# Token tiles of a fused linear-attention and gMLP kernel: transposed by TensorE, or loaded transposed and centred by an adding transfer

## The chip, the cores and the metric

The kernel runs on one NeuronCore of a Trainium2 chip. The metric is device time in microseconds (us), from the first instruction to the last with what lies around it. The kernel before takes 641.28 us (median of 3 runs, 640.76 to 642.08).

Five engines run side by side, each in its own fixed order: TensorE (PE in the profile, with its weight loads as PEld), VectorE (DVE), ScalarE (ACT), GpSimd (POOL) and SyncE (SP), which only issues transfers. GpSimd and ScalarE also issue transfers. An instruction waits on semaphores of other engines and of transfers, and everything behind it on its engine waits with it.

## The reference

One layer of 2048 tokens with 512 features, in float32. Cut to what matters:

```python
x  = A_x                                          # [1, 2048, 512]
xn = layernorm(x)                                 # per token: (x - mean) / sqrt(var + 1e-5)
out = x + A(xn) + B(xn)

def A(x):                                         # linear attention, 32 heads of 16
    q, k, v = split(x @ wqkv)
    pq, pk  = per_head(q) @ w_phi, per_head(k) @ w_phi
    phi_q = concat(softmax(pq), softmax(-pq));  phi_k likewise
    kv, z = phi_k^T v, sum over tokens of phi_k
    return ((phi_q kv) / (phi_q z + 1e-6)) @ wo

def B(x):                                         # gated MLP over tokens
    z1, z2 = halves(gelu(x @ w_in))               # 688 columns each
    g = w_sp @ layernorm(z2) + b_sp               # [2048, 2048] over the tokens
    return (z1 * g) @ w_out
```

## The kernel before, in words

Tokens are cut into 16 tiles of 128. Every product is made in three passes of float32r numbers (a high part times a high part, high times low, low times high: `mm3`, lines 50 to 53), so each operand is split into a high part `h` (a rounding copy, line 43) and a rest `l` (a subtraction, line 47).

The first stage, up to about 225 us, is where the change lies. For each tile `s` it needs the tile transposed (features on the 128 partitions) and with each token's mean taken off; the factor 1/sqrt(var) is applied later, to the outputs. A tile goes through these steps:

- `fetch` (line 176 by way of `load_x`): SyncE loads `xt`, tokens on partitions. Five buffers (`XB`).
- `stats` (lines 249, 250): VectorE finds mean and variance of each token.
- `center` (lines 254 to 256): GpSimd makes `nm`, the negative mean, and r = 1/sqrt(var + eps) (lines 84, 85); ScalarE adds `nm` to `xt`.
- `transposed` (line 268): four 128x128 transposes on TensorE into a PSUM bank `pt`.
- `split_x`: ScalarE rounds `pt` to the high part of `xT` (line 43), VectorE takes the rest (line 47).

Tiles 0 to 3 are done in a hand-written prologue, with the loading and folding of the weights. A loop over `s` does the others. Pass `s` of the loop has the projection to keys `proj` of tile `s` (12 matrix multiplications of 128x512), the softmax pair `softmax_k` on it (lines 103 to 113: max and min, two subtractions, `Exp` on ScalarE, sum, reciprocal), `normalise` (lines 285, 286: VectorE scales the features `e`, and GpSimd issues a transfer that adds them to `zacc`), the projection to values of tile `s + 1`, statistics and centring of tile `s + 3`, a projection to queries with its softmax pair whose result GpSimd writes to `e_d` (line 281), and a projection `zps` for the gated MLP (line 140). After each even `s`, `run` puts the transposes of tiles `s + 2` and `s + 3` and then the products `kvps` of features and values (line 293) on TensorE, and after them the two splits. Key, value and query projections and the transposes share four PSUM banks (tag `mm`).

The order on each engine is set by the program's own scheduler from its cost estimates; `issue_after` binds some instructions behind others. The input `x_t`, the tokens in transposed blocks, is an argument of the kernel before as well, which does not read it.

Behind the first stage come the rest of the MLP projections, a Strassen-like product over the tokens (`g`, from about 290 to 500 us), and the output projections. They are the same in both kernels.

Of the kernel before, what the change touches and what calls it, by code (L numbers as in the profile page):

```python
# [10 lines left out]
F32 = mybir.dt.float32  # L11
# [7 lines left out]
P = 128  # L19
# [10 lines left out]
XB = 5  # L30
# [5 lines left out]
def mixer(ctx: ExitStack, tc: tile.TileContext, x, x_t, wv, wqkT, phi_bd, wo, w_in, wst, b_r, w_out, out):  # L36
# [34 lines left out]
    zb_d = dram.tile([P, NF], F32, name="zb_d")  # L71

# [8 lines left out]
    def rstd_of(mv, r, stats=None):  # L81
        if stats is not None:
            dve.bn_aggr(mv, stats)
        pool.tensor_scalar_add(mv[:, 1:2], mv[:, 1:2], EPS_LN)
        pool.tensor_tensor(r, mv[:, 1:2], mhalf, op=ALU.pow)
# [83 lines left out]
    with ExitStack() as p0:  # L169
# [87 lines left out]

        def centered_on_dve(s):
            stats(s)
            ins = dve.tensor_scalar(xt[s], xt[s], mv_x[:, s, 0:1], None, op0=ALU.subtract).ins  # L260
            rstd_of(mv_x[:, s], r_x[:, s:s + 1])
            return ins
# [20 lines left out]
        def normalise(er):  # L283
            e = er[:, :NF]
            dve.tensor_tensor(heads(e), heads(e), bc(er[:, NF:], 2 * H), op=ALU.mult)
            pool.dma_start(zacc, e, accum_op=ALU.add)
            return e
# [9 lines left out]
        def run(tiles, feats):  # L297

            with ExitStack() as order:
                for i in ahead_of_run:  # L300
                    order.enter_context(tc.issue_after(i))
                ahead_of_run.clear()
                pts = []
                for t in tiles:
                    pt, i = transposed(t)
                    pts.append(pt)
                    order.enter_context(tc.issue_after(i))
                for t, e in feats:
                    i = add_kv(t, e)
            for pt in pts:  # L310
                split_x(pt)
            return i
# [9 lines left out]
        fetch(4)  # L322
        w1r = load_rows(w_in[:, :FH], FH)
        sp.dma_start(bias, b_r)
# [75 lines left out]
        for s in range(NT):  # L400
            if s:
                fetch(s + 4)
            er = ek if s == 0 else softmax_k(s, p1 if s == 1 else proj(s, wqk_h[:, 1], wqk_l[:, 1]))
            ahead_of_run.append(proj.last)
            feats.append((s, normalise(er)))
            if 0 < s < NT - 1:
                ahead_of_run.append(proj_v(s + 1)[0])
            if 0 < s < NT - 3:
                with tc.issue_after(shifted):
                    stats(s + 3)  # L410
                with tc.issue_after(z1_raw.last if s % 2 and s > 1 else q_half):
                    center(s + 3)
# [13 lines left out]
            if s and s % 2 == 0:  # L426
                last = run([t for t in (s + 2, s + 3) if t < NT], feats[:-1])
# [527 lines left out]
```

## Time and profile before

| | |
|---|---|
| median of 3 runs | 641.28 us (640.76 to 642.08) |
| the profiled execution | 639.98 us, of which the span 638.3 us |
| TensorE busy | 632.3 us, 99% of the span |
| VectorE busy | 507.1 us, 79% |
| ScalarE busy | 273.4 us, 43% |
| GpSimd busy | 105.7 us, 17% |
| granted TensorE clock | full in all 40 slices of the span |

How to read it: the span is one execution, taken by the hardware profiler. A group line of the profile gives the source line, engine, operation and tile names (output <- inputs), how often it ran, busy time and mean duration, then the idle time in front of it and what ended that. A timeline row gives start and duration in us. A transfer's issue is a short instruction on the engine that issues it; its landing is told apart. Instructions of VectorE and ScalarE overlap by some 0.1 us at their ends, so steps between starts are a little shorter than durations.

### The profile page before, as it was taken

Reading aid. Unit: us, or ns where it says so; the run is one execution under the profiler, and the core shown is the slowest. Engines: PE = TensorE matmul, PEld = TensorE weight load, DVE = VectorE, ACT = ScalarE, POOL = GpSimd, SP = SyncE. Lnnn points to the kernel's source line nnn. Section 1 sums busy time; section 2 is a strip of 40 time slices with the busy share of each in tenths; the row PEclk is TensorE's granted clock in tenths of the full one; section 3 lists DMA queues with packets and bytes.
Section 4 is the critical chain, followed back from the end, with each engine's and each line's share of the span. In section 5 each row is a group of like instructions: output and inputs, shape, how many; then the busy total and the mean of one; then the engine's idle time right before and its main releaser. Section 6 shows DMA issues by size and latency. Waiting matters only on the chain.

```text
span 638.3 us, 11615 instructions
## 1 busy us (share of the span) xinstructions
PE 632.3 (99%) x4511; PEld 574.9 (90%) x4511; DVE 507.1 (79%) x919; ACT 273.4 (43%) x457; POOL 105.7 (17%) x194
## 2 busy tenths in 40 slices
PE   8999999999999999999999999999999999999997
PEld 6898888888888999999999999999999887888886
DVE  6979789888978579889988778687796698989521
ACT  5533433343332447887534434434343433223330
POOL 4532211212101005432010010100101200001000
PEclk9999999999999999999999999999999999999999
DMA  8363543534453851002453443533548877775620
GB/s 334 120 163 82 148 141 96 163 106 109 126 170 91 275 195 67 0 2 67 135 193 102 146 148 104 178 125 118 163 149 273 278 264 246 259 278 194 240 68 33
DMA packets 38519, 98.15 MB, mean 154 GB/s; under 512 B 4832, under 2 KB 6368, under 8 KB 38464
## 3 DMA queue, kind: packets, MB, share of 16 engines
q1 hardware_dynamic: 26720, 55.46, 27.0%
q0 software_dynamic: 9152, 35.79, 18.1%
q10 hardware_dynamic: 2592, 6.16, 2.5%
q8 instruction: 35, 0.57, 0.4%
q14 instruction: 20, 0.16, 0.1%
HBM read 56.24 MB, written 26.48 MB: 130 GB/s over the span
## 4 chain that ended last, share of the span: by engine, by line
PE 97%; DMA 2%; DVE 0%; SPq 0%; ACT 0%; issue 0%; POOL 0%
PE g L53 11%; PE g L52 11%; PE g L51 11%; PE proj L51 7%; PE proj L52 7%; PE proj L53 7%; PE zps L51 6%; PE zps L53 6%; PE zps L52 6%; PE pout L51 6%; PE pout L52 5%; PE pout L53 5%; PE ptq L828 1%; PE po L842 1%; PE kvps L293 1%; PE pout L860 1%
## 5 line engine op out<-in xcount | busy, mean ns | idle before, releaser
L53 PE MATMUL g<-B,A 128*128 128x344 f32 x448 | 143.4, 320 | 0.0
L52 PE MATMUL g<-B,A 128*128 128x344 f32 x448 | 143.3, 320 | 0.0
L51 PE MATMUL g<-B,A 128*128 128x344 f32 x448 | 143.3, 320 | 0.0
L53 PEld LDWEIGHTS g<-B,A 128*128 128x128 f32 x448 | 84.2, 188 | 0.1
L51 PEld LDWEIGHTS g<-B,A 128*128 128x128 f32 x448 | 84.2, 188 | 0.0
L52 PEld LDWEIGHTS g<-B,A 128*128 128x128 f32 x448 | 84.2, 188 | 0.0
L43 ACT ACTIVATE A<-S 128x512 fp32r<-128x512 f32 x64 | 39.9, 630 | 61.9 <-PE g L53 32.6
L47 DVE TENSOR_TENSOR A<-S,A 128x512 fp32r<-128x512 f32 x64 | 43.6, 687 | 27.6 <-ACT A L43 27.1
L110 ACT ACTIVATE e<-e,r_x 128x1024 f32<-128x1024 f32 x32 | 36.8, 1150 | 50.0 <-DVE e L109 34.8
L112 DVE TENSOR_REDUCE sm<-e 128x64 f32<-128x1024 f32 x32 | 38.7, 1210 | 15.0 <-ACT e L110 15.0
L51 PE MATMUL proj<-wqk_h,xT 128*128 128x512 f32 x124 | 49.6, 400 | 0.0
L52 PE MATMUL proj<-wqk_l,xT 128*128 128x512 f32 x124 | 48.7, 393 | 0.0
L53 PE MATMUL proj<-wqk_h,xT 128*128 128x512 f32 x124 | 48.7, 393 | 0.0
L43 ACT ACTIVATE A<-wf 128x512 fp32r<-128x512 f32 x64 | 33.3, 520 | 34.3 <-PE g L53 29.1
L47 DVE TENSOR_TENSOR A<-wf,A 128x512 fp32r<-128x512 f32 x64 | 35.4, 553 | 9.8 <-ACT A L43 9.3
L51 PE MATMUL zps<-w_h,xT 128*128 128x344 f32 x128 | 41.8, 326 | 0.0
L53 PE MATMUL zps<-w_h,xT 128*128 128x344 f32 x128 | 40.9, 319 | 0.0
L52 PE MATMUL zps<-w_l,xT 128*128 128x344 f32 x128 | 40.8, 319 | 0.0
L140 ACT ACTIVATE z1f<-zps,r_x 128x344 f32<-128x344 f32 (+1 forms) x29 | 16.5, 576 | 40.4 <-PE zps L53 37.8
L51 PE MATMUL pout<-wu,uh 128*128 128x512 f32 (+1 forms) x80 | 31.6, 395 | 0.0
L52 PE MATMUL pout<-wu,uh 128*128 128x512 f32 (+1 forms) x80 | 30.4, 380 | 0.0
L53 PE MATMUL pout<-wu,ul 128*128 128x512 f32 (+1 forms) x80 | 30.4, 380 | 0.0
(197 smaller groups left out, 1461.5 us busy)
## 6 DMA issues: line engine op xcount, KB each, us to landing
wf<-in_wst SPq DMA_DIRECT2D x64, 256.0 KB, 3.3
e_d<-e POOLq DMA_DIRECT2D x16, 544.0 KB, 3.2
et<-e_d SPq DMA_DIRECT2D x16, 544.0 KB, 5.6
zacc<-e POOLq DMA_DIRECT2D x16, 512.0 KB, 4.6
er<-et POOLq DMA_DIRECT2D x12, 512.0 KB, 3.9
u_d<-z1t POOLq DMA_DIRECT2D x16, 368.0 KB, 4.9
u<-u_d SPq DMA_DIRECT2D x15, 368.0 KB, 4.7
z_d<-z1f ACTq DMA_DIRECT2D x16, 344.0 KB, 4.0
```

The lines of the kernel that those rows point to most:

```text
L43: return act.activation(h, src, AF.Copy).ins
L47: return (eng or dve).tensor_tensor(l, src, h.bitcast(F32), op=ALU.subtract).ins
L51: pe.matmul(dst, ah, bh, start=start, stop=False)
L52: pe.matmul(dst, ah, bl, start=False, stop=False)
L53: return pe.matmul(dst, al, bh, start=False, stop=stop).ins
L110: act.activation(e, e, AF.Exp, scale=scale)
L112: dve.tensor_reduce(sm, heads(e), axis=AX.X, op=ALU.add)
L140: z1_raw.last = act.activation(z[:, k], p, AF.Copy, scale=r_x[:, s:s + 1]).ins
L293: ins = pe.matmul(kv_acc[k:k + QP, m // 4], vs[:, m * QP:(m + 1) * QP], e[:, m * HP:(m + 1) * HP], start=s == 0 and m < 4, stop=s == NT - ...
L828: pe.transpose(pt[:, a, k].bitcast(F32R), src, ident_r)
L842: lasts[3] = pe.matmul(po[r][c * QP:(c + 1) * QP, j // NG], kvT[rows, j], fs[j // 2][rows, j % 2], start=True, stop=True).ins
L860: pe.matmul(p, rt, w[:, ds], start=False, stop=False)
```

## The change

From the fifth tile on (tiles 4 to 15), the tile is no longer transposed and centred on the chip's engines:

- `fetch_T` loads the tile twice: `xt` as before, for the statistics alone (three buffers now), and `raw` from `x_t`, already in transposed blocks (two buffers, the pool's default).
- `mean_out` (in place of `center`): GpSimd makes the negative means `nm` and writes them, 128 numbers, to `nm_d` in device memory.
- `mean_in`: after the transfer that adds the features to `zacc`, GpSimd issues a second adding transfer. It reads the row of 128 means for each of 128 partitions and 4 blocks and adds it to `raw`.
- `split_x` then splits `raw` (in SBUF) instead of `pt` (in PSUM), one tile a pass, two tiles ahead.
- `run` has only the products `kvps`; the 48 transposes of tiles 4 to 15 and the 12 centrings on ScalarE are gone.

```diff
-XB = 5
+XB = 3
...
+    nm_d = dram.tile([NT, P], F32, name="nm_d")
...
-        pool.tensor_tensor(r, mv[:, 1:2], mhalf, op=ALU.pow)
+        return pool.tensor_tensor(r, mv[:, 1:2], mhalf, op=ALU.pow).ins
...
+        raws = {}
+
+        def fetch_T(s):
+            if s < NT:
+                fetch(s)
+                raws[s] = wk.tile([P, ND, P], F32, tag="raw", name="raw")
+                sp.dma_start(raws[s], x_t[s])
+
+        def mean_out(s):
+            stats(s)
+            xt.pop(s)
+            nm = wk.tile([P, 1], F32, tag="nm", name="nm")
+            pool.tensor_scalar_mul(nm, mv_x[:, s, 0:1], -1.0)
+            pool.dma_start(nm_d[s:s + 1, :].rearrange("a p -> p a"), nm)
+            return rstd_of(mv_x[:, s], r_x[:, s:s + 1])
+
+        def mean_in(s):
+            pool.dma_start(raws[s], nm_d[s:s + 1, :].unsqueeze(1).to_broadcast([P, ND, P]), accum_op=ALU.add)
+
...
-            pool.dma_start(zacc, e, accum_op=ALU.add)
+            normalise.last = pool.dma_start(zacc, e, accum_op=ALU.add).ins
...
-        def run(tiles, feats):
+        def run(feats):
...
-                pts = []
-                for t in tiles:
-                    pt, i = transposed(t)
-                    pts.append(pt)
-                    order.enter_context(tc.issue_after(i))
                 for t, e in feats:
                     i = add_kv(t, e)
-            for pt in pts:
-                split_x(pt)
             return i
...
-        fetch(4)
         w1r = load_rows(w_in[:, :FH], FH)
+        fetch_T(4)
...
         for s in range(NT):
-            if s:
-                fetch(s + 4)
             er = ek if s == 0 else softmax_k(s, p1 if s == 1 else proj(s, wqk_h[:, 1], wqk_l[:, 1]))
             ahead_of_run.append(proj.last)
+            if 1 < s < NT - 2:
+                with tc.issue_after(shifted):
+                    split_x(raws.pop(s + 2))
+            if s:
+                fetch_T(s + 4)
             feats.append((s, normalise(er)))
             if 0 < s < NT - 1:
                 ahead_of_run.append(proj_v(s + 1)[0])
             if 0 < s < NT - 3:
                 with tc.issue_after(shifted):
-                    stats(s + 3)
-                with tc.issue_after(z1_raw.last if s % 2 and s > 1 else q_half):
-                    center(s + 3)
+                    mean_out(s + 3)
+                with tc.issue_after(normalise.last):
+                    mean_in(s + 3)
...
-                last = run([t for t in (s + 2, s + 3) if t < NT], feats[:-1])
+                last = run(feats[:-1])
```

The scheduler moves the instructions with it. Three places matter below. In each, rows are source line, operation, output <- inputs and the shape.

VectorE in the fourth and fifth pass, from the scaling of the key features of tile 4 (L285 before, L305 now) to those of tile 5. Before:

```order
L285 TENSOR_TENSOR e<-e 128x1024
L47 TENSOR_TENSOR xT<-pt,xT 128x512 x2
L112 TENSOR_REDUCE sm<-e 128x64
L103 TENSOR_REDUCE mm<-proj 128x32
L113 RECIPROCAL e<-sm 128x64
L104 TENSOR_REDUCE mm<-proj 128x32
L108 TENSOR_TENSOR e<-proj,mm 128x32x16
L109 TENSOR_TENSOR e<-mm,proj 128x32x16
L249 BN_STATS st_1021<-xt 128x6
L250 BN_AGGR mv_x<-st_1021 128x2
L112 TENSOR_REDUCE sm<-e 128x64
```

The same place in the change, as far as the sum over the key features of tile 5:

```order
L305 TENSOR_TENSOR e<-e 128x1024
L113 TENSOR_REDUCE sm<-e 128x64
L104 TENSOR_REDUCE mm<-proj 128x32
L105 TENSOR_REDUCE mm<-proj 128x32
L114 RECIPROCAL e<-sm 128x64
L109 TENSOR_TENSOR e<-proj,mm 128x32x16
L110 TENSOR_TENSOR e<-mm,proj 128x32x16
L250 BN_STATS st_1024<-xt 128x6
L251 BN_AGGR mv_x<-st_1024 128x2
L47 TENSOR_TENSOR xT<-raw,xT 128x512
L113 TENSOR_REDUCE sm<-e 128x64
```

Two splits of `pt` stood right behind the scaling in every second pass; now one split of `raw` (tile 7 here) stands in every pass, behind the statistics and ahead of the sum over this pass's key features. On ScalarE the rounding half of that split stands ahead of the `Exp` that this sum reads.

GpSimd in the same pass, from the negative means of one tile to the write of the query features. Before:

```order
L254 TENSOR_SCALAR nm<-mv_x 128x1
L84 TENSOR_SCALAR mv_x<-mv_x 128x1
L85 TENSOR_TENSOR r_x<-mv_x,mhalf 128x1
L286 DMA zacc<-e 128x1024
L281 DMA e_d<-e 128x1088
```

The same in the change:

```order
L271 TENSOR_SCALAR nm<-mv_x 128x1
L85 TENSOR_SCALAR mv_x<-mv_x 128x1
L272 DMA nm_d<-nm 128x1
L86 TENSOR_TENSOR r_x<-mv_x,mhalf 128x1
L306 DMA zacc<-e 128x1024
L276 DMA raw<-nm_d 128x4x128
L301 DMA e_d<-e 128x1088
```

The write of the means comes in behind `nm`, and the adding transfer to `raw` directly behind the one to `zacc`.

TensorE at the first of these tiles, from the end of the key projection of tile 3 to the value projection of tile 4. Before:

```order
L53 MATMUL proj<-wqk_h,xT 128x512
L51 MATMUL proj<-wv_h,xT 128x512
L52 MATMUL proj<-wv_l,xT 128x512
L51 MATMUL zps<-w_h,xT 128x344
L52 MATMUL zps<-w_l,xT 128x344
L53 MATMUL zps<-w_h,xT 128x344
L51 MATMUL zps<-w_h,xT 128x344
L52 MATMUL zps<-w_l,xT 128x344
L53 MATMUL proj<-wv_h,xT 128x512
```

The same in the change:

```order
L53 MATMUL proj<-wqk_h,xT 128x512
L51 MATMUL proj<-wv_h,xT 128x512
L52 MATMUL proj<-wv_l,xT 128x512
L53 MATMUL proj<-wv_h,xT 128x512
L51 MATMUL proj<-wv_h,xT 128x512
```

The five multiplications of the MLP projection that stood inside the value projection are now in one block with the rest of theirs, later.

## The prediction, made before the result was known

> **What bounds the kernel now.** I read the page's busy shares and its chain of waits first, then the first stage by windows, then row by row.
>
> ```profile
> span 638.3 us, 11615 instructions
> PE 632.3 (99%) x4511; PEld 574.9 (90%) x4511; DVE 507.1 (79%) x919; ACT 273.4 (43%) x457; POOL 105.7 (17%) x194
> PE 97%; DMA 2%; DVE 0%; SPq 0%; ACT 0%; issue 0%; POOL 0%
> ```
>
> TensorE carries 97% of the chain: a matrix instruction that goes is worth its place, and a wait costs its length. The ten passes from the key projection of tile 3 to that of tile 13 (columns: window, length, busy us of PE, PEld, DVE, ACT, POOL, clock, share of the DMA engines, GB/s), and TensorE at their ends:
>
> ```profile
> 43.04:168.71 125.67, 125.67 (x919) 107.72 (x913) 110.72 (x167) 48.48 (x65) 24.89 (x48) 1.00 0.46 128
> ...
> 41.04 1.04 PE L268 MATMUL pt<-ident,xt 128*128 128x128 f32 x8
> 42.01 1.10 PE L293 MATMUL kvps<-e,v 128*32 128x64 f32 x64
> 43.04 0.50 PE L51 MATMUL proj<-wqk_h,xT 128*128 128x512 f32 x1
> ...
> 168.71 0.50 PE L51 MATMUL proj<-wqk_h,xT 128*128 128x512 f32 x1
> ```
>
> TensorE is busy in all of it: 12.57 us a pass. VectorE has 110.72 of 125.67 us, 88%, so 1.5 us a pass are free on it; ScalarE is idle most of the time. TensorE waits for nobody here, but VectorE is the engine that would hold it next. One pass of VectorE, and the rows by which the steps are priced:
>
> ```profile
> 46.13 0.69 DVE L103 TENSOR_REDUCE mm<-proj 128x32 f32<-128x512 f32 x1 [1.92 <-PE proj L53]
> 46.74 0.68 DVE L104 TENSOR_REDUCE mm<-proj 128x32 f32<-128x512 f32 x1
> 47.33 0.68 DVE L108 TENSOR_TENSOR e<-proj,mm 128x512 f32<-128x512 f32 x1
> 47.93 0.68 DVE L109 TENSOR_TENSOR e<-mm,proj 128x512 f32<-128x512 f32 x1
> 48.52 0.69 DVE L249 BATCH_NORM_STATS2 st<-xt 128x6 f32<-128x512 f32 x1
> 49.25 0.18 DVE L250 BATCH_NORM_AGGREGATE mv_x<-st 128x2 f32<-128x6 f32 x1
> 49.87 1.22 DVE L112 TENSOR_REDUCE sm<-e 128x64 f32<-128x1024 f32 x1 [0.44 <-ACT e L110]
> 51.13 0.55 DVE L113 RECIPROCAL e<-sm 128x64 f32<-128x64 f32 x1
> 51.71 1.23 DVE L285 TENSOR_TENSOR e<-e 128x1024 f32<-128x1024 f32 x1
> 52.86 0.68 DVE L103 TENSOR_REDUCE mm<-proj 128x32 f32<-128x512 f32 x1
> ...
> 48.69 1.15 ACT L110 ACTIVATE e<-e,r_x 128x1024 f32<-128x1024 f32 x1 [5.31 <-issue]
> ```
>
> From start to start a reduction or subtraction takes 0.6 us, the statistics 0.75, a sum 1.15, a reciprocal 0.5, the scaling (normalise) 1.2; the `Exp` 1.15 on ScalarE.
>
> **The change, part by part.** *TensorE, removed.* Eight transposes hold their place for 42.01 - 41.04 = 0.97 us; six such groups (tiles 4 to 15) make 5.8 us, and a pass becomes 12.57 - 0.49 = 12.1 us. *ScalarE and VectorE, removed.* Twelve centrings on ScalarE, and splits that read SBUF in place of PSUM. Both engines have idle time beside TensorE, so this is worth nothing by itself; if VectorE were the bound, the splits would give 12 x 0.13 us (the rows below). *SyncE, added.* Twelve loads of 256 KB more. Tile `xt` takes 4.6 us to land, 6.9 at worst; `raw` is issued some 0.5 us after the statistics of its tile begin (it stands behind an `xt` load that waits for them), and the add that needs it is issued 8 us after. Cost nothing; without that cover up to the excess over 7.5 us a pass.
>
> ```profile
> L43 ACT ACTIVATE A<-wf 128x512 fp32r<-128x512 f32 x64 | 33.3, 520 | 34.3 <-PE g L53 29.1
> L47 DVE TENSOR_TENSOR A<-wf,A 128x512 fp32r<-128x512 f32 x64 | 35.4, 553 | 9.8 <-ACT A L43 9.3
> L43 ACT ACTIVATE xT<-pt x16: 580/591/617, 6.5 to 167.9; 128x512 fp32r<-128x512 f32 x16
> L47 DVE TENSOR_TENSOR xT<-pt,xT x16: 658/680/692, 7.2 to 170.5; 128x512 fp32r<-128x512 f32 x16
> DMA to landing us min/median/max: 3.1/4.6/6.9
> ```
>
> *GpSimd, added.* The write of the means is issued some 5 us before the scaling ends and lands before the add is issued (as a transfer such as `e_d` it takes 3.2 us); its issue is short. Nothing in the steady passes, and 0.57 us ahead of the first `zacc` at 33.23.
>
> *The wait that is added.* This decides. The add to `raw` can be issued only after the transfer of `normalise`, on the same queue. VectorE's split of `raw` waits for its landing, and behind it stands the rest of the pass. ScalarE's half waits too, and behind it stands the `Exp` of this pass's keys.
>
> ```profile
> 33.23 1.06 POOL L286 DMA_DIRECT2D zacc<-e  x1
> 38.56 0.90 POOL L286 DMA_DIRECT2D zacc<-e  x1 [3.64 <-ACT e L110]
> 44.75 0.94 POOL L286 DMA_DIRECT2D zacc<-e  x1 [4.03 <-DVE xT L47]
> 53.47 0.95 POOL L286 DMA_DIRECT2D zacc<-e  x1 [2.74 <-DVE e L285]
> ...
> e_d<-e POOLq DMA_DIRECT2D x16, 544.0 KB, 3.2
> zacc<-e POOLq DMA_DIRECT2D x16, 512.0 KB, 4.6
> out<-xr SPq DMA_DIRECT2D x15, 256.0 KB, 2.1
> out<-xr SPq DMA_DIRECT2D x2, 128.0 KB, 1.7
> ...
> q1 hardware_dynamic: 26720, 55.46, 27.0%
> q0 software_dynamic: 9152, 35.79, 18.1%
> ```
>
> The price of an add to `raw`: scaling ends at 51.71 + 1.23 = 52.94, `zacc` is issued at 53.47, 0.53 later, and lands 4.6 after that. Plain, 128 KB more cost 0.4 us (2.1 - 1.7), 512 KB thus 1.6; the adding one lands 1.4 later than `e_d` of the same size, so its bytes cost 3.0, and the 256 KB of the add 1.5, behind `zacc` on the queue. 0.53 + 4.6 + 1.5 = 6.6 us; with something for 512 pieces in place of 128 and for the other traffic I take **7.0 us from the end of the scaling to the landing**. Bounds: 4.6 if the add does not queue behind `zacc` (0.53 + 0.95 for the issue in front + 4.6 - 1.5); 17.1 if a piece of 512 B costs what a 4 KB piece of `zacc` does (0.53 + 4.6 + 4 x 3.0). Packets' time has so far gone by bytes: q1 has 0.270 x 638.3 x 16 / 55.46 = 50 us per MB with 2 KB packets, q0 52 with 4 KB. So I stay near the low end.
>
> One pass with it, in full (scaling of tile 4 to scaling of tile 5, from the order quoted above). VectorE's work ahead of the split: sum 1.15, two reductions 1.2, reciprocal 0.5, two subtractions 1.2, statistics 0.75, together 4.8 us. The add lands at 7.0, ScalarE's half is done at 7.6 (0.1 + 0.52), its `Exp` at 8.7, then VectorE: sum, two reductions, reciprocal, two subtractions, scaling, 5.25 in all: **14.0 us, against TensorE's 12.1**. Where more work stands between scaling and split (tiles 6 and 11, with 8 to 9 us) nothing is lost; tiles 10, 12, 14, 15 (some 6.5 to 7.2) lose little; tiles 5, 7, 8, 9, 13 (3.7 to 5.2) lose 2 to 3 us.
>
> What takes this up is lead: a split is needed one to two passes later, by the value projection. I laid the rows out with these prices, TensorE with 2.77 us a projection, 3.77 a `zps`, 1.03 a `kvps`. Tile 4 first: `zacc` transfers follow each other by their landings (44.75 - 38.56 = 6.2); the second comes at 38.56 + 0.57 = 39.1, lands at 45.3, the add 1.6 behind, ScalarE's half at 47.5, where TensorE wants it at 41.04 + 1.03 + 2.77 = 44.8.
>
> ```
> tile  scaling before it ends  add lands  high part  wanted at  TensorE waits
>  4            -                 46.9       47.5       44.8        2.6
>  5            -                 51.9       52.5       58.5        0
>  6          57.8                64.8       65.4       68.8        0
>  7          69.4                76.4       77.0       80.9        0
>  8          83.5                90.5       91.1       94.0        0
>  9          97.6               104.6      105.2      105.0        0.3
> 10         110.5               117.5      118.1      119.3        1.4
> 11         127.5               134.5      135.1      132.0        3.2
> 12         138.6               145.6      146.2      148.3        0
> 13         149.6               156.6      157.2      159.4        0.4
> 14         163.6               170.6      171.2      172.8        0
> 15         178.7               185.7      186.3      184.9        1.5
> ```
>
> (The 1.4 and 0.4 are PSUM banks: the second subtraction that frees one stands behind a split.) Sum of waits 9.4, transposes 5.8: the span grows by 3.6 to 641.9. The profiled execution took 639.98 for a span of 638.3, and the median is 641.28, 2.98 over the span: **644.9 us**.
>
> In the Trainium skill, "TensorE: Matmul & The Clock Gate" (Part 1: The HAM clock gate), the clock halves after an idle window of about 3.4 us; no wait of the trace of before is that long (the clock is full throughout), and it would add some 1.7 us here, an estimate from that page, only where the wait for tile 11 grew past that.
>
> **The rivals.**
>
> *The add is hidden.* If its landing comes within about 6 us of the scaling, a pass on VectorE stays under 12.5 us, the lead lasts to the end, and at the low bound of 4.6 us no wait is left: 641.28 - 5.8 = 635.5; with 2 us for tile 4, 637.5. For it: VectorE has 1.5 us a pass free; my chain ignores that its instructions overlap, some 0.3 us a pass. Against it: one queue, and two adding transfers behind each other on it. By the Trainium skill, "DMA: Bandwidth & Descriptors" (Anatomy of one DMA), a transfer from GpSimd takes about 2.0 us and its bytes over 436 GB/s, 2.6 us here, an estimate from that page that would give this rival; for `zacc` the same rule gives 3.2 where the trace has 4.6.
>
> *Even.* A landing between 6.2 and 6.7 us: waits of 4.5 to 7 us eat the 5.8: 640 to 642.5.
>
> *The pieces decide.* 512 pieces of 512 B, all read from one row of device memory, which no transfer of this trace does. At half of the high bound's piece price the add takes 6 us in place of 1.5, lands at 11.5, each of some ten passes takes 18.5 in place of 12.1; after the lead of some 5 us the rest is paid: about 641 - 6 + 60 - 5 = 690. At a quarter (3 us, landing at 8.5) the waiting passes take 15.5, and the sum is near 655. For it: nothing here has such small pieces. Against it: time by bytes, above.
>
> **How the numbers follow.** Forecast (landing 6.7 to 8.5, slower, its own range 642.6 to 655): 0.48. Hidden: 0.29. Even: 0.13. Pieces (over 655): 0.10. Within 0.2%, 640.0 to 642.6, a measurement of this kernel cannot be told from no change. Faster 0.29, same 0.13, slower 0.58. The range takes in the hidden add and leaves out most of the pieces: 635.5 to 656.
>
> **What would show it.** TensorE's busy time falls by 5.8 us and 48 instructions in any case. Right: idle time of TensorE before `proj` of tile 4 and in later value projections, put down to ScalarE's or VectorE's `xT`; VectorE's split of `raw` waiting 2 to 3 us in passes 3, 5, 6, 7; the add landing 6 to 7 us after its `zacc` is issued. Wrong: no idle time on TensorE beyond the 2 us of before, and the split waiting less than 1 us; or landings of over 10 us. I would be most wrong in the price of the add: one microsecond of it moves the sum by some 5 us.

## The result, and the profile after

The change makes the kernel slower: 705.7 us (median of 6 runs, 701.8 to 707.1) against 641.1 us (6 runs, 640.4 to 642.1), a ratio of 1.100 (95% interval 1.097 to 1.103). The forecast was 644.9 us, 635.5 to 656: the direction was right, and the size was missed by a factor of seventeen in the difference (64.6 us against 3.8). Times are medians over all executions but one, of `f1_add_first`, which took 1573.7 us where its three others took 752.4 to 753.7.

The page of the change: span and instructions, busy times, the 40 slices of TensorE's busy share and of its granted clock, and the chain of waits.

```profile
span 700.1 us, 11582 instructions
PE 648.3 (93%) x4463; PEld 581.3 (83%) x4463; DVE 509.2 (73%) x919; ACT 264.7 (38%) x445; POOL 129.8 (19%) x218
...
PE   8979977577968699999999999999999999999998
...
PEclk9999998899988899999999999999999999999999
...
PE 65%; DMA 9%; DVE 4%; ACT 1%; issue 1%; POOL 0%; POOLq 0%; ACTq 0%; DVEq 0%
```

Three things are new beside the span: TensorE has idle slices in the first 40% only, its clock is below full in that part alone, and it has 65% of the chain in place of 97%. Though 48 instructions (5.8 us) are gone from TensorE, its busy time rose from 632.3 to 648.3 us. The span splits without a rest: idle time 700.1 - 648.3 = 51.8 us against 6.0 before (+45.8); longer busy time 648.3 - (632.3 - 5.8) = 21.8; transposes -5.8. Together 61.8 us, the difference of the two spans. Of the 21.8, the clock makes some 19: 37.7 us of the busy time lie in ten stretches in which the granted clock is 0.50.

By windows (start and end, length, busy us of PE, PEld, DVE, ACT, POOL, clock, share of the DMA engines, GB/s), from 43 us, ahead of the first value projection that waits (at 52.45), to the end of the first stage, and from there to the end; the change first, then the kernel before:

```profile
43.00:291.00 248.00, 203.63 (x1384) 169.44 (x1383) 157.28 (x240) 65.86 (x93) 52.24 (x78) 0.91 0.63 134
291.00:700.00 409.00, 405.91 (x2679) 380.39 (x2678) 317.16 (x626) 178.21 (x320) 54.42 (x100) 1.00 0.46 153
```

```profile
43.00:229.00 186.00, 186.00 (x1357) 161.38 (x1350) 157.47 (x241) 71.03 (x99) 31.08 (x57) 1.00 0.51 146
229.00:638.00 409.00, 405.81 (x2678) 380.14 (x2676) 316.09 (x623) 178.27 (x320) 54.22 (x100) 1.00 0.46 153
```

The whole loss lies in the first stage: 186 us have become 248, and the 409 us behind it are the same. VectorE does the same work in it (157 us): it isn't slower, it waits. The waits of the change (engine and line, what for: us in total, times, longest):

```profile
ACT xT L43 <- DMA raw<-nm_d: 113.2, 12, 13.4
...
PE proj L51 <- ACT xT L43: 26.7, 8, 6.1
...
PE proj L51 <- ACT v L293: 17.6, 3, 8.2
```

All twelve splits on ScalarE wait for the adding transfer, 9.4 us on average; VectorE's halves wait for ScalarE's (8.19 us in the timeline below); TensorE pays the end of it. (The `v` at L293 is what ScalarE has to do behind the split before a PSUM bank comes free.) One pass, from the scaling of one tile's key features to the next split, by the timeline:

```profile
98.34 1.22 DVE L305 TENSOR_TENSOR e<-e 128x1024 f32<-128x1024 f32 x1
...
100.11 0.93 POOL L306 DMA_DIRECT2D zacc<-e  x1 [13.07 <-ACT e L111]
100.74 1.67 POOL L276 DMA_DIRECT2D raw<-nm_d  x1
...
111.99 0.63 ACT L43 ACTIVATE xT<-raw 128x512 fp32r<-128x512 f32 x1 [11.81 <-DMA raw<-nm_d]
112.53 1.13 ACT L111 ACTIVATE e<-e,r_x 128x1024 f32<-128x1024 f32 x1
112.65 0.69 DVE L47 TENSOR_TENSOR xT<-raw,xT 128x512 fp32r<-128x512 f32 x1 [8.19 <-ACT xT L43]
```

The order is the one that the prediction laid out: scaling, `zacc`, add, split on ScalarE, `Exp` behind it, VectorE's half. The scaling ends at 99.56, `zacc` is issued 0.55 later, and the split begins at 111.99: **12.4 us** where the prediction has 7.0. Over the twelve tiles it is 11.7 to 14.2. A pass takes 19.3 us (81.43, 100.74 and 120.01 are issues of three adds in a row).

The transfers of the change (KB each, median us from issue to landing), to be set beside `e_d` 3.2, `zacc` 4.6 and `xt` 4.6 of the kernel before:

```profile
e_d<-e POOLq DMA_DIRECT2D x16, 544.0 KB, 7.6
...
zacc<-e POOLq DMA_DIRECT2D x16, 512.0 KB, 4.9
...
xt<-in_x SPq DMA_DIRECT2D x16, 256.0 KB, 5.9
...
raw<-in_x_t SPq DMA_DIRECT2D x12, 256.0 KB, 6.3
raw<-nm_d POOLq DMA_DIRECT2D x12, 256.0 KB, 11.0
...
nm_d<-nm POOLq DMA_DIRECT2D x12, 0.5 KB, 10.7
```

Two rows stand out: the add of 256 KB lands after 11.0 us, though `zacc`, twice its size and also adding, takes 4.9; and the write of 512 bytes of means takes 10.7. The profile cannot say what makes either slow. The experiments are about that.

### The profile page after: what moved, and what is told of

Read it like the earlier page. It is cut to its first block, busy times and chain, and to the rows that moved or that the text cites. A ratio compares the mean times of both kernels' runs of the same rounds, so it can differ in the third digit from the quotient of the medians.

```text
span 700.1 us, 11582 instructions
## 1 busy us (share of the span) xinstructions
PE 648.3 (93%) x4463; PEld 581.3 (83%) x4463; DVE 509.2 (73%) x919; ACT 264.7 (38%) x445; POOL 129.8 (19%) x218
## 4 chain that ended last, share of the span: by engine, by line
PE 65%; DMA 9%; DVE 4%; ACT 1%; issue 1%; POOL 0%; POOLq 0%; ACTq 0%; DVEq 0%
PE g L53 10%; PE g L52 10%; PE g L51 10%; DMA raw<-nm_d 9%; PE pout L51 5%; PE pout L52 5%; PE pout L53 5%; PE zps L51 4%; PE zps L53 4%; PE zps L52 4%; PE ptq L844 1%; PE po L858 1%; PE pout L876 1%; DVE sm L113 1%; PE proj L51 1%
## 5 line engine op out<-in xcount | busy, mean ns | idle before, releaser
L51 PE MATMUL proj<-wv_h,xT 128*128 128x512 f32 x60 | 29.9, 499 | 40.2 <-ACT xT L43 26.7
L47 DVE TENSOR_TENSOR xT<-raw,xT 128x512 fp32r<-128x512 f32 x12 | 8.3, 692 | 78.5 <-ACT xT L43 78.5
L43 ACT ACTIVATE A<-S 128x512 fp32r<-128x512 f32 x64 | 40.0, 631 | 61.4 <-PE g L53 36.3
L51 PE MATMUL proj<-wqk_h,xT 128*128 128x512 f32 x124 | 51.0, 411 | 4.2 <-ACT v L293 4.2
L51 PEld LDWEIGHTS proj<-wv_h,xT 128*128 128x128 f32 x60 | 14.6, 244 | 47.3 <-ACT xT L43 30.2
L43 ACT ACTIVATE xT<-raw 128x512 fp32r<-128x512 f32 x12 | 7.6, 629 | 113.2 <-DMA raw<-nm_d 113.2
L52 PE MATMUL proj<-wqk_l,xT 128*128 128x512 f32 x124 | 50.2, 405 | 0.0
L53 PE MATMUL proj<-wqk_h,xT 128*128 128x512 f32 x124 | 50.1, 404 | 0.0
L43 ACT ACTIVATE A<-wf 128x512 fp32r<-128x512 f32 x64 | 33.4, 521 | 37.7 <-PE g L53 31.6
## 6 DMA issues: line engine op xcount, KB each, us to landing
wf<-in_wst SPq DMA_DIRECT2D x64, 256.0 KB, 3.3
```

The lines of the kernel that those rows point to most:

```text
L43: return act.activation(h, src, AF.Copy).ins
L47: return (eng or dve).tensor_tensor(l, src, h.bitcast(F32), op=ALU.subtract).ins
L51: pe.matmul(dst, ah, bh, start=start, stop=False)
L52: pe.matmul(dst, ah, bl, start=False, stop=False)
L53: return pe.matmul(dst, al, bh, start=False, stop=stop).ins
```

## The experiments

Each is an edit of the change, but for `i3_before_writes`, an edit of the kernel before. Code is cut to the lines that matter. Ratios are to the kernel before on the same chip, with their 95% intervals; its median there was 640.6 to 641.0 us.

**First: what about the add is slow?** Four theories: its 512 pieces are too small; all pieces read the same 512 bytes of device memory; the adding is slow; or something else holds the first stage, and not the add.

`e3_512_rows`: 512 pieces of 512 B as before, each from a row of its own.

```diff
-            pool.dma_start(raws[s], nm_d[s:s + 1, :].unsqueeze(1).to_broadcast([P, ND, P]), accum_op=ALU.add)
+            pool.dma_start(raws[s], x[:ND*P, :P].rearrange("(a p) b -> p a b", p=P), accum_op=ALU.add)
```

> The add takes 512 pieces of 512 B again, but each from a row of its own (the first 128 numbers of 512 rows of x; what is added is not the mean). Pieces theory: nothing changes, landing 10 to 12 us, 698 to 712 us. One-row theory: it lands like an add of 256 KB, 6.5 to 7.5 us after its issue, 640 to 655 us.

`e2_rows_2k`: 128 pieces of 2 KB, all from one row of `x` (here as in e3 other numbers than the means are added, and in e1 none).

```diff
+            pool.dma_start(raws[s].rearrange("p a b -> p (a b)"), x[s * P:s * P + 1, :].to_broadcast([P, D]), accum_op=ALU.add)
```

> The add takes 128 pieces of 2 KB, all read from one row of x of 512 numbers, in place of 512 pieces of 512 B from one row of nm_d (what is added is not the mean). Same bytes, same place on the queue, still one row of device memory. Pieces theory (a piece costs the queue the same whatever its size): a quarter of the pieces, so the add lands about 6.5 to 7.5 us after its issue in place of 11.0, and the time falls to 640 to 655 us, my own sum. One-row theory (reads of one row stand behind each other) and order theory (two adding transfers behind each other are late whatever their pieces): landing 10 us or more, 690 us or more.

`e4_plain`: the transfer of the change without the addition.

```diff
-            pool.dma_start(raws[s], nm_d[s:s + 1, :].unsqueeze(1).to_broadcast([P, ND, P]), accum_op=ALU.add)
+            pool.dma_start(raws[s], nm_d[s:s + 1, :].unsqueeze(1).to_broadcast([P, ND, P]))
```

> The same 512 pieces of 512 B from the one row of nm_d, but as a plain transfer over raw, without the add (the splits then get the means alone). Pieces theory, pieces of any transfer: nothing changes, 698 to 712 us. Adding theory (what is slow is a small piece that adds): it lands earlier than 11.0 us, at 6 to 8 us after its issue, 640 to 660 us.

`e1_no_add`: no add at all.

```diff
-            pool.dma_start(raws[s], nm_d[s:s + 1, :].unsqueeze(1).to_broadcast([P, ND, P]), accum_op=ALU.add)
+            pass
```

> The add to raw is left out (so the means are not taken off from the fifth tile on); the loads of raw, the writes of nm_d, the statistics and the splits stay. If the add's landing is all that costs, the transposes' 5.8 us are left over: 641.1 - 5.8 = 635.3 us, from 634 to 638. If one of the edits priced at nothing (twelve loads more on SyncE, the writes of nm_d on the queue of GpSimd, splits of raw that take 629 and 692 ns) holds TensorE too, the time stays over 640 us.

Measured: e3 673.0 us (1.0505, 1.0489 to 1.0520), e2 670.3 (1.0463, 1.0446 to 1.0481), e4 702.5 (1.0964, 1.0945 to 1.0983), e1 656.8 (1.0238, 1.0199 to 1.0278). The add's row in the profiles of e3, e2 and e4, in this order:

```profile
raw<-in_x POOLq DMA_DIRECT2D x12, 256.0 KB, 9.4
```

```profile
raw<-in_x POOLq DMA_DIRECT2D x12, 256.0 KB, 7.5
```

```profile
raw<-nm_d POOLq DMA_DIRECT2D x12, 256.0 KB, 10.6
```

As many pieces of the same size from 512 rows take 33 us less than from one row: the repeated reading of the same 512 bytes is a cause, and small pieces alone are not. Going on from 512 pieces of 512 rows to 128 pieces of one 2 KB row is worth 2.7 us (e3 less e2); since two things change there, this doesn't price the pieces by themselves. The adding is worth 3.2 us by the medians (705.7 less e4), but the executions of the two kernels overlap, so it may be nothing. But all three stay some 30 us or more above the kernel before; the repeated row is not all of it. e1 isn't the clean floor that it was meant to be: with no add to wait for, the scheduler put ScalarE's splits earlier, where they wait for the loads of `raw` instead (`ACT xT L43 <- DMA raw<-in_x_t: 47.4, 10, 11.0`). The fastest of those loads land 2.6 us after their issue, but the two behind the longest waits after 12.1 and 10.5; GpSimd issued a write of means 1.4 us behind each of these two (54.87 and 56.26 us, 81.38 and 82.76). The fourth series is about that.

**Second: the queue, or the row?** The add stands behind `zacc` on one queue. `f1_add_first` issues it right behind the write of the means, ahead of `zacc`; `f2_row4` makes the row 2 KB (four times the means, written as 512 numbers in place of 128); `f3_both` does both; `f4_one_piece` shrinks the add to one piece of 512 B, so that nearly all of `raw` keeps its mean.

```diff
f1, f3:
                     mean_out(s + 3)
-                with tc.issue_after(normalise.last):
                     mean_in(s + 3)
f2, f3:
+    nm_d = dram.tile([NT, ND * P], F32, name="nm_d")
...
+            pool.dma_start(nm_d[s].rearrange("(c p) -> p c", p=P), nm.to_broadcast([P, ND]))
...
+            pool.dma_start(raws[s].rearrange("p a b -> p (a b)"), nm_d[s:s + 1, :].to_broadcast([P, D]), accum_op=ALU.add)
f4:
+            pool.dma_start(raws[s][:1, 0, :], nm_d[s:s + 1, :], accum_op=ALU.add)
```

> The add stands ahead of the pass's zacc transfer on the queue of GpSimd in place of behind it; its 512 pieces of one row stay. Order theory (an add behind zacc is late): it lands about 7 us after its own issue in place of 11.0 and is issued some 2 us earlier, so the splits wait little: 640 to 660 us. One-row theory alone (what is late is the reading of one row, wherever it stands): landing still 9 us or more, 680 us or more.

> The means are written four times side by side, so that the add takes 128 pieces of 2 KB from a row of 2 KB, with the right numbers; behind zacc as in the change. One-row theory (reads of the same 512 B stand behind each other, and a row four times as long has four such places): as the run with a row of x, 665 to 675 us, landing 7 to 8 us. If the write of 512 single numbers costs the queue something: over 680 us.

> Both: row of 2 KB, and the add ahead of zacc. If the landing of the add is all that costs: it lands 3 to 4 us after its issue, before the next pass wants it; the transposes' gain is left, 635 to 641 us. If the loads of raw (6.3 us to landing where xt took 4.6) or the waits of the queue's head for nm_d hold the passes too: 645 us or more.

> The add takes one piece of 512 B (the first partition of raw alone, so the other means are not taken off), in the same place behind zacc, so every wait and the order stay and its bytes go. By my sum a landing of 5 to 6 us after the issue costs little: 636 to 645 us. If the place behind zacc costs by itself more than the sum had (a clock that falls in each wait, ScalarE's work behind the split, late loads of raw): 650 to 668 us.

Measured: f1 753.2 us (1.1749, 1.1729 to 1.1769), f2 677.9 (1.0579, 1.0552 to 1.0606), f3 714.8 (1.1138, 1.1107 to 1.1168), f4 668.5 (1.0430, 1.0406 to 1.0453). f2 saves 28 us, as the one-row theory has it, and does so with the kernel's own means, though it writes four times as many numbers. Issuing the add ahead of `zacc` makes both forms some 37 to 48 us slower, and f3's waits tell why (for f1, which has no trace of an execution of 753 us, this is inferred):

```profile
POOL raw L276 <- DMA nm_d<-nm: 63.0, 8, 8.8
```

```profile
raw<-nm_d POOLq DMA_DIRECT2D x12, 256.0 KB, 4.7
...
nm_d<-nm POOLq DMA_DIRECT2D x12, 2.0 KB, 9.6
```

The add itself now lands 4.7 us after its issue, but GpSimd stands waiting for the *write of the means* to land, and `zacc` behind it waits too. The prediction had that write at nothing in the passes. f4 shows the other side: a transfer of 512 bytes behind `zacc` still lands 6.6 us after its issue (`raw<-nm_d POOLq DMA_DIRECT2D x12, 0.5 KB, 6.6`), and the kernel is 28 us slower than before with hardly an add in it.

**Third: more lead.** If waits for late transfers are all, issuing them a pass earlier or splitting later should hide them. `g2_late` puts the splits behind the scaling of their pass; `g1` and `g4` also take statistics and write a pass earlier and free the add from its place behind `zacc`, with the 2 KB row (g4 with a third `raw` buffer and one `xt` buffer less).

```diff
+                with tc.issue_after(normalise.scaled):
+                    split_x(raws.pop(s + 2))
... g1, g4 as well:
+            if s < NT - 3:
+                with tc.issue_after(shifted):
+                    mean_in(s + 3) if s else mean_out(4)
...
+                    if s < NT - 4:
+                        mean_out(s + 4)
```

> One thing of the change is moved: the split of raw (both halves, and with them the next load into that buffer) stands behind the pass's scaling in place of behind its second subtraction of the keys, so ScalarE's Exp and VectorE's scaling of that pass no longer stand behind it. The add is as in the change, 512 pieces of one row, behind zacc. Waiting-pass theory (what costs is that the split stands in the middle of the chain of VectorE and ScalarE, so landing plus the rest of the chain is longer than TensorE's pass): the add now has a whole pass of 12 us to land, waits mostly go, 640 to 665 us. Landing theory (the add is late for the value projection itself): 690 us or more.

> The late split, and beside it a row of 2 KB for the add (means written four times) and the means a pass earlier. The add lands 7.5 to 8.5 us after its issue and the split comes a pass later: 635 to 645 us. If the load of raw, which can start only after the late split of the tile two before, is what is late then: 650 us or more.

> As the run before it, with three buffers for raw in place of two (two for xt in place of three; tile 2 of x comes into a buffer of raw), so that the load of raw is there a pass earlier. If nothing but the transposes is left of the change: 635 to 638 us, faster than before. If it is over 641 us, ScalarE's and VectorE's order or the transfers' traffic still hold TensorE.

Measured: g2 686.5 us (1.0715, 1.0694 to 1.0735), g1 692.1 (1.0795, 1.0766 to 1.0823), g4 694.8 (1.0852, 1.0804 to 1.0901). None comes near the kernel before. In g1 the adds did not come earlier: GpSimd waits 40.9 us for loads of `raw` ahead of them (`POOL raw L276 <- DMA raw<-in_x_t: 40.9, 6, 9.6`). g2's timeline shows a flaw of the edit:

```profile
77.94 0.63 ACT L43 ACTIVATE xT<-raw 128x512 fp32r<-128x512 f32 x1 [9.74 <-DMA raw<-nm_d]
...
79.05 1.14 ACT L111 ACTIVATE e<-e,r_x 128x1024 f32<-128x1024 f32 x1
```

Binding the split behind an instruction of VectorE moved only VectorE's half; on ScalarE the split still stands ahead of the `Exp`. So `h2_pin` binds ScalarE's half behind the `Exp` of its pass and VectorE's behind the scaling, and `h1_pin_row4` does the same with the 2 KB row. ("The run before it" in what was expected of h2 is h1.)

```diff
+            exp_k = softmax_pair.exp
...
             feats.append((s, normalise(er)))
+            if 1 < s < NT - 2:
+                split_x(raws.pop(s + 2), exp_k, normalise.scaled)
```

> As the run before it, but with the change's own add: 512 pieces of the one row of 512 B, landing 11 to 12 us after its issue, 12 to 13 us after a scaling. Place theory: ScalarE's half waits some 3 us in each pass, with only evictions behind it, which TensorE's banks cover in part: 640 to 655 us. If one row costs as much here as in the change (33 us): 670 us or more.

> Both halves of the split are put behind the chain they held up: ScalarE's half behind the Exp of the keys of its pass, VectorE's behind the scaling of its pass; the row of the means is 2 KB (written four times). Nothing else of the change is moved. Place theory (what costs is that Exp and scaling stand behind a split that waits for the add): the add is issued about 1.2 us after a scaling, lands 8.3 us later, and ScalarE reaches the split some 9 to 10 us after that scaling, so the waits are gone but for tile 4: 635 to 643 us. Late-add theory (TensorE's value projection wants the tile before the add can have landed): 665 us or more.

Measured: h2 671.0 us (1.0457, 1.0436 to 1.0478), h1 674.9 (1.0540, 1.0504 to 1.0577). The right place of the splits is worth 35 us (705.7 to 671.0) with the 512 B row. But the 2 KB row, worth 28 us in the change's own order (f2), now is worth nothing, and the add lands after 11.4 us in h1 though it is the fast form. (h1 also writes four times as many numbers; those writes land after 14.5 us.) Something else slows the transfers.

**Fourth: the writes of the means.** Each is 128 (in f2, h1: 512) separate 4-byte numbers to device memory. `i3_before_writes` puts the twelve writes into the kernel before, where nobody reads them. `i1_no_write` is the change without them (`nm_d` is filled with zeros once, so no mean is taken off), and `i2_pin_row4_no_write` is h1 without them, with zeros too.

```diff
i3 (against the kernel before):
+            if s > 3:
+                pool.dma_start(nm_d[s:s + 1, :].rearrange("a p -> p a"), nm)
i1 (against the change):
+    pool.dma_start(nm_d, zacc[:NT, :P])
...
-            pool.dma_start(nm_d[s:s + 1, :].rearrange("a p -> p a"), nm)
i2 (against h1):
+    pool.dma_start(nm_d, zacc[:NT, :ND * P])
...
-            pool.dma_start(nm_d[s].rearrange("(c p) -> p c", p=P), nm.to_broadcast([P, ND]))
```

> The kernel before, and beside it the twelve writes of the negative means to nm_d, which nobody reads. Write theory: zacc lands later than 4.6 us and xt later than 4.6 us in the median, by 1 us or more, and the time is 642 to 655 us as far as VectorE and ScalarE wait for tiles. If the writes are harmless: 640 to 642 us, landings as before.

> The change without its writes of the means: nm_d is filled with zeros once at the start, and the add reads those (no mean is taken off from the fifth tile on). Adds, loads and order stay. Write theory (a write of 128 numbers of 4 B holds up the transfers of all queues for some 5 us): zacc and raw land earlier, the add some 3 us earlier (8 to 9 us in place of 11.0), 660 to 690 us. If the writes cost nothing, as I predicted: 700 to 710 us.

> The run with both halves of the split behind Exp and scaling and a row of 2 KB (675 us), without the writes: nm_d is zeros, written once. Write theory: no transfer stands still, the add lands within a pass, 635 to 645 us. If not: 665 to 680 us.

Measured: i3 644.5 us (1.0058, 1.0045 to 1.0071), i1 703.4 (1.0982, 1.0966 to 1.0998), i2 637.2 (0.9952, 0.9936 to 0.9967). The transfers of i3 show the second cause alone, in a kernel that has no add and no `raw`:

```profile
e_d<-e POOLq DMA_DIRECT2D x16, 544.0 KB, 6.2
...
zacc<-e POOLq DMA_DIRECT2D x16, 512.0 KB, 6.0
...
xt<-in_x SPq DMA_DIRECT2D x16, 256.0 KB, 6.7
...
nm_d<-nm POOLq DMA_DIRECT2D x12, 0.5 KB, 9.2
```

Twelve writes of 512 bytes, 6 KB in all, make the other transfers land up to twice as late (3.2, 4.6 and 4.6 without them), those of SyncE's queue too, and `z_d` on ScalarE's (7.0 us against 4.0). A median mixes transfers beside a write with others. Those that were issued between 66.5 and 69.6 us of i3, with the write, show it better:

```profile
e_d<-e POOLq DMA_DIRECT2D x1, 544.0 KB, 11.7
xt<-in_x SPq DMA_DIRECT2D x2, 256.0 KB, 11.0
z_d<-z1f ACTq DMA_DIRECT2D x1, 344.0 KB, 10.9
nm_d<-nm POOLq DMA_DIRECT2D x1, 0.5 KB, 10.6
```

Transfers of three queues land within 1.6 us of each other, at the time of the write; `e_d` had been issued 1.2 us ahead of it.

The 3.7 us that i3 costs don't come from these landings, though: TensorE waits for no transfer in it. Its one new wait stands in the prologue:

```profile
30.10 4.55 DVE L288 TENSOR_TENSOR e<-e 128x1024 f32<-128x1024 f32 x1
...
36.44 0.43 PE L51 MATMUL zps<-w_h,xT 128*128 128x344 f32 x1 [1.80 <-DVE wqk_l L47]
```

The issue of the first write, 0.79 us on GpSimd, stands ahead of GpSimd's splits of weights. Beside these, a scaling on VectorE takes 4.55 us where the kernel before has 2.05 (why isn't shown). A split of weights behind it comes late, and TensorE waits 1.80 us and then runs 3.4 us at half clock: some 3.5 us in all. The change has the same wait (1.79 us, at 35.39), and so have e2, e3, e4, f2, f4, g2, h1 and h2; the kernel before, i1, i2, j1 and k1, which write no means in the loop, have none.

Without the writes, h1 falls by 38 us to 637.2, below the kernel before. That the add has to wait for its own write is not the reason: in the change and in h1, every write of which the trace tells the landing had landed 1.6 us or more before the add that reads it was issued. The page of i2, where the add lands after 6.4 us (`raw<-nm_d POOLq DMA_DIRECT2D x12, 256.0 KB, 6.4`):

```profile
span 635.0 us, 11581 instructions
PE 627.2 (99%) x4463; PEld 569.2 (90%) x4463; DVE 507.6 (80%) x919; ACT 266.4 (42%) x445; POOL 118.6 (19%) x207
```

i1 shows that the two causes hide each other: with the one row of 512 B still read, the add lands after 11.0 us with and without the writes, and the writes are worth 2.3 us, less than the executions of each kernel differ and no more than the wait in the prologue.

**Last: the sum with the landing that it assumed.** `k1_row4_no_write` has the change's own order, splits ahead of the `Exp`, with the 2 KB row and no writes (`nm_d` holds zeros, as in i1).

> The change with a row of 2 KB for the add, and without the writes of the means (nm_d is zeros, written once, so no mean is taken off from the fifth tile on); the split stands where the change has it. The add should land 6.4 us after its issue as in the last run with such a row and no writes, 7.6 us after the scaling, 0.6 more than the 7.0 of my sum. If the sum was right but for that price: 644.9 + 0.6 x 5 = 648 us, from 644 to 652. If its model of the passes is too kind (TensorE's clock falls in the waits, ScalarE's evictions stand behind the split): 655 us or more. If the place costs nothing once the traffic is gone: 637 us, as with the split behind Exp and scaling.

Measured: 648.8 us (1.0130, 1.0108 to 1.0152). Its page, the waits of TensorE for the first stage, and the pass:

```profile
span 647.9 us, 11581 instructions
PE 631.2 (97%) x4463; PEld 569.8 (88%) x4463; DVE 507.2 (78%) x919; ACT 264.6 (41%) x445; POOL 118.6 (18%) x207
```

```profile
PE proj L51 <- DVE e L110: 4.6, 3, 2.1
PE proj L51 <- ACT xT L43: 3.6, 3, 1.6
PE proj L51 <- ACT v L293: 2.7, 1, 2.7
```

```profile
98.14 1.22 DVE L305 TENSOR_TENSOR e<-e 128x1024 f32<-128x1024 f32 x1
...
107.19 0.63 ACT L43 ACTIVATE xT<-raw 128x512 fp32r<-128x512 f32 x1 [7.78 <-DMA raw<-nm_d]
```

Here the split begins 7.8 us after the scaling ends (7.2 to 8.1 from tile 6 on), near the 7.0 of the prediction, TensorE waits 10.9 us for projections, where the prediction has 9.4, and the time is 3.9 us over the forecast.

**A version that beats both.** `j1_product` keeps the transposed loads and does without both costs: ScalarE writes the tile's means on the diagonal of a 128x128 block, one product with a block of ones spreads them over the partitions of a PSUM bank, and VectorE subtracts that from `raw`. No write of means, no add. The splits stand in pairs again, after each even `s`, as in the kernel before. Shown against the change:

```diff
-            pool.dma_start(nm_d[s:s + 1, :].rearrange("a p -> p a"), nm)
...
-            pool.dma_start(raws[s], nm_d[s:s + 1, :].unsqueeze(1).to_broadcast([P, ND, P]), accum_op=ALU.add)
...
+            i = act.activation(dg, ident, AF.Copy, scale=mv_x[:, s, 0:1]).ins
...
+            return pm[:, :P], pe.matmul(pm[:, :P], ones, dgs.pop(s), start=True, stop=True).ins
...
+            dve.tensor_tensor(raw, raw, pm.unsqueeze(1).to_broadcast([P, ND, P]), op=ALU.subtract)
+            split_x(raw)
...
+                last = run([t for t in (s + 2, s + 3) if t < NT], feats[:-1])
```

> The transposed loads stay, but the means come neither by a write nor by an add: ScalarE makes a diagonal of a tile's means (128x128), one product of TensorE with ones spreads them over the partitions, VectorE subtracts them from raw (0.68 us more a tile). TensorE has 12 products in place of 48 transposes, some 4 us less: 636 to 639 us, faster than before, if the loads of raw alone are harmless. If the loads themselves stop the other transfers, or VectorE (then some 11.7 us of a pass of 12.2) becomes the bound: 643 us or more.

Measured: 637.1 us (6 runs, 636.9 to 639.8), ratio 0.9951 (0.9936 to 0.9966). The page, and by tile the product and the subtraction (min, median, max in ns):

```profile
span 635.4 us, 11621 instructions
PE 629.4 (99%) x4487; PEld 572.7 (90%) x4487; DVE 513.9 (81%) x931; ACT 270.7 (43%) x457; POOL 102.7 (16%) x182
```

```profile
L283 PE MATMUL pm<-xt,ones x24: 271/275/275, 41.1 to 164.9; 128*128 128x128 f32 x24
L287 DVE TENSOR_TENSOR raw<-raw,pm x12: 631/680/689, 41.6 to 167.2; 128x512 f32<-128x512 f32 x12
```

Each product has two rows in the trace. TensorE is busy 2.9 us less than before (the transposes' 5.8 less 2.9, or 0.24 us a tile, for the products), and nothing waits in its place. The subtraction on VectorE, twelve times 0.68 us, is hidden.

## Why the prediction was right or wrong, point by point

How each version's span comes about, from its page (busy time compared with 632.3 - 5.8 = 626.5):

| | span | TensorE idle | busy over 626.5 | of that, by a halved clock |
|---|---|---|---|---|
| the change | 700.1 | 51.8 | 21.8 | 18.8 |
| k1: 2 KB row, no writes | 647.9 | 16.7 | 4.7 | 1.7 |
| i2: k1 with the splits behind the `Exp` | 635.0 | 7.8 | 0.7 | 0 |

The last column is half of TensorE's busy time in the stretches with a granted clock of 0.50. What makes up the rest of the busy time over 626.5, some 3 us in the change and in k1, isn't traced.

- **The step that failed: the price of the add's landing.** The prediction priced it at 7.0 us from the end of the scaling and argued "Packets' time has so far gone by bytes" and "So I stay near the low end". It measured 11.7 to 14.2 in the change. No transfer of the kernel before reads one row many times, so bytes could not price this one. Of the pass of 19.3 us, the 6.9 from the split's start to the end of the next scaling are what the prediction has (7.0): this term alone was mis-sized, by 5 us a pass. With the 2 KB row and no writes the landing comes after 7.2 to 8.1, and the time is 648.8, where the forecast's 644.9, by its own 5 us per us of landing, becomes some 648. That they agree so closely is in part luck: the waits for projections came near (10.9 us, 9.4 in the sum), but the 4.7 us of longer busy time were not in the sum.
- **The second step that failed: the write of the means "lands before the add is issued (as a transfer such as `e_d` it takes 3.2 us)".** It does land before the add is issued, but it takes 9 to 11 us, and transfers under way beside it land with it (i3), so that "Nothing in the steady passes" is wrong. In the passes of the change this is hidden behind the first step (i1), and its place ahead of the first `zacc`, 0.57 us in the prediction, costs some 3.5; with the 2 KB row it is worth 22 us (e2, whose writes are the change's, less k1) to 29 us (f2, with four times as many numbers, less k1).
- **The rival "the pieces decide"** came nearest in its numbers: landing 11.5, pass 18.5, 690 us, against 12.4, 19.3, 706. Of its two halves, "512 pieces of 512 B" and "all read from one row", the second carries the weight: with 512 rows 33 us are saved; what the pieces cost by themselves no run tells. It had 0.10, and the range left most of it out, since the argument by bytes was used against it though no row could test it.
- **The place of the wait was right**: splits on both engines, the `Exp` behind ScalarE's half, the sum behind that, first wait of the loop at the value projection of tile 4 (3.70 us, at 52.45). k1 against i2 prices the place itself: moving the splits behind the `Exp` and the scaling is worth 11.5 us.
- **The transposes' gain was right** in sign, and the rival "hidden" (635.5 to 637.5) is what i2 (637.2) and j1 (637.1) reach, once the landing is hidden or the add is gone. Its chance of 0.29 was given to the change as it stands, which did not reach it.
- **The raw loads "cost nothing" is right, if only without the writes:** in j1 SyncE loads as many tiles (6.0 us to land) and TensorE waits for none of them; with the writes some came late (e1, up to 12.1 us).
- **The clock was left out of the sum,** since no wait was to be long. In the change some 19 of the 61.8 us are the clock. TensorE after a wait of 4.02 us:

```profile
93.39 0.50 PE L51 MATMUL proj<-wv_h,xT 128*128 128x512 f32 x1 [4.02 <-ACT xT L43]
...
95.13 0.63 PE L52 MATMUL proj<-wv_l,xT 128*128 128x512 f32 x1
95.56 0.63 PE L53 MATMUL proj<-wv_h,xT 128*128 128x512 f32 x1
...
97.63 0.39 PE L52 MATMUL proj<-wv_l,xT 128*128 128x512 f32 x1
97.86 0.40 PE L53 MATMUL proj<-wv_h,xT 128*128 128x512 f32 x1
```

  Matrix multiplications start 0.43 us apart for some 2.5 us and 0.23 apart from 97.6 on, so the projection costs 4.7 us in place of 2.77: 2 us on top of the wait. In the Trainium skill, "TensorE: Matmul & The Clock Gate" (Part 1: The HAM clock gate), the clock halves after an idle window of about 3.4 us and comes back after as long a busy one. The traces agree on the factor and the length: each stretch of the change is 3.4 or 6.8 us long at 0.50, and each of its nine waits of 3.1 to 8.2 us in the loop has one, which costs 1.9 us on average. They don't agree that TensorE must be idle for so long: a wait of 1.80 us in i3 and one of 2.12 in k1 (at 168.48) are each followed by 3.4 us at half clock, while one of 2.75 in k1 (at 109.48) isn't.
- **Wrong and without effect:** the splits from SBUF were to be faster (520 and 553 ns, from those of the weights). They take 629 and 692 ns in the change, longer than those from PSUM before (591 and 680).

What stays open: why one row of device memory, read 512 times by one transfer, is slow (the trace shows how long packets take, not where in the memory they wait), and how a write of single numbers holds up transfers on other queues. i1 shows that the row needn't be freshly written to be slow, since there it was filled once, ahead of the loop. That the 55 us between i1 and k1 are the repeated row rather than the fewer pieces is shown with the writes present only (e3 against the change), not without them.

## What to carry to other kernels

A transfer that spreads one short row over all partitions, or that writes one number per partition to device memory, is not priced by its bytes: look for the same access pattern in a trace before giving it a price, and where there is none, let the range reach to the bound. When several engines' work stands behind such a transfer, first ask what else can carry the value: here a product with ones did the same for 0.24 us of TensorE a tile. And when a wait on TensorE may reach some 3 us, count about 2 us more for the clock behind it; it came behind a wait of 1.8 and one of 2.1 us as well.

## What the runs showed of the hardware that was not expected

- 256 KB that read the same 512 bytes 512 times, issued behind `zacc`, land 10.6 to 12.7 us after their issue in the median, adding or not, with the writes or without (e4, the change, i1, g2, h2); 9.4 from 512 rows (e3), 7.5 to 11.4 from one row of 2 KB (e2, f2, h1), and 6.4 from that once no means are written (i2, k1).
- A write of 128 single float32 numbers from 128 partitions to device memory lands after 9 to 11 us, alone in a kernel without the rest too (9.2), and transfers of 256 to 544 KB on three queues land 1.4 to 3 us later in the median of that kernel; those under way beside a write land with it, some 11 us after their issue. In the Trainium skill, "DMA: Bandwidth & Descriptors" (Specifications), a transfer below 512 B makes the engine read, modify and write; the direction agrees, but the page gives no price, and no run here shows that this is the mechanism.
- Two causes of this kind don't add up: one alone removed gives 2 us (less than the executions differ) or 28, both give 57 (705.7 less 648.8). An experiment that removes one suspect and finds nothing has not acquitted it.
